# Chunked attention, a balanced mixture of experts and a float64 second layer on one core: weights are loaded two decodes ahead and decoded in even steps, the head hands over its x operands a step later, and the operands move by 352 bytes

## The chip, the cores and the metric

The kernel runs on one core of a Trainium2 chip. The metric is device time in microseconds (us) from the first to the last instruction and the little that lies around them; lower is better. Three runs of the kernel before stand beside one profiled execution of it.

## The reference

Three stages follow one another. Attention works in chunks of 64 positions; its output, as 2304 tokens of 512 features, goes through eight experts with a weight for every token and expert that eight rounds of row and column normalisation balance; a last layer takes the maximum of three products.

```python
def _attn_ref(q, k, v):                      # (4, 8, 576, 64), chunks of 64
    scores = scale * np.matmul(q_c, k_c.transpose(0, 1, 2, 4, 3))
    attn = np.exp(scores - scores.max(-1, keepdims=True))
    return np.matmul(attn / (attn.sum(-1, keepdims=True) + 1e-09), v_c)

def _moe_ref(x, w_gate, w1, w2):             # x (2304, 512), 8 experts, hidden 1024
    logits = x @ w_gate
    P = np.exp(logits - logits.max())
    for _ in range(8):
        P /= P.sum(1, keepdims=True) + 1e-09
        P /= P.sum(0, keepdims=True) + 1e-09
        P *= N / E
    for e in range(E):
        out += P[:, e:e + 1] * (np.maximum(x @ w1[e], 0.0) @ w2[e])

def _moe2_ref(x, w1, w2, w3, w_out):         # hidden 768
    h = np.maximum(np.maximum(x @ w1, x @ w2), x @ w3)
    return h @ w_out
```

The weights of the last layer (`wts2` in the kernel) reach the chip as 64-bit words, which are float64 numbers; the kernel decodes them itself into a high and a low float32 part.

## The kernel before

Every product is made of three matmuls of float32r halves: high by high, high by low, low by high (`wh`, `wl` for weights, `xh`, `xl` for tokens, `hh`, `hl` for hidden values). The first product of a layer is Strassen-like: seven products (`PRODUCTS`) in place of eight, so one item of work has 42 matmuls of 128x384 (line 235). The second product (`down`, line 267) has 36 matmuls of 128x512 for an expert item: six output tiles, each evicted by VectorE into `acc`.

An **item** is a pair of hidden blocks of an expert for a third of the tokens ("M"), or one of nine pieces of the last layer ("m"). The phases run in the order M0, M1, m0, M2, m1, m2 with 32, 32, 9, 32, 9 and 9 items, numbered through as n = 0 to 122. Within an item the seven products are the **positions** 0 to 6. After each position the main loop issues, in order of the code, the prepared side work of that place (the table `bg`, filled by `at(n, pos, f)`), then at position 1 the weight fetch of a later item (`fetch`, lines 166 to 170), and then one output tile of the item before. At position 2 `fetch2` (line 178) comes ahead of the side work. Every engine runs its own instructions strictly in that order, and all transfers are issued by SP, one after another: an entry of SP's queue that waits holds all behind it.

In the first 49 us, the **head**, a loop over k = 0 to 7 makes attention for the first six tiles: scores (`s`), exponentials (`e`), normalisation (lines 491 to 494), transposes on TensorE (`tp`), the product with v (`xp`), and from each two tiles an `x_head` call, which makes 128 columns of `xh` and `xl`. `warm` issues matmuls on ones, whose result nobody reads.

Side work that the change touches: `fold_all` (items 22 to 30) loads 30 stored partial sums (`u`) three steps ahead and adds them into `acc` (line 322). `decode_all` makes the operands of the last layer from the float64 words in 24 jobs during items 33 to 62: one or two loads of `w`, three empty steps, ten arithmetic steps on VectorE (first reader of `w` is line 383, tile `sc`), the high half `dhi` by ScalarE, the low half `dlo` by GpSimd, and two stores of them into `scr` (line 423) or `scro` (line 437). Ten steps fall into one item. From item 33 on, a third buffer for `wh` and `wl`, in the pool `late` at the other end of the memory, serves every third item.

Of the kernel before, what the change touches and what calls it, by code (L numbers as in the profile page):

```python
# [47 lines left out]
def kernel(ctx: ExitStack, tc: tile.TileContext, qk, vv, wg, wts, wts2, out):  # L48
# [24 lines left out]
    cp.tile([P, 392], F32, name="gap")  # L73
# [239 lines left out]
    def fold_all():  # L313
        jobs = [(e, t) for e in range(NRAW) for t in range(TS)]
        got = {}
        for i in range(len(jobs) + 3):
            if i < len(jobs):
                got[i] = big[0].tile([P, DM], F32, name="u", tag="u", bufs=4)
                nc.sync.dma_start(out=got[i], in_=up_part[jobs[i]])
            if i >= 3:  # L320
                e, t = jobs[i - 3]
                nc.vector.scalar_tensor_tensor(out=acc[t], in0=got.pop(i - 3), scalar=Pt[:, t, e:e + 1],
                                               in1=acc[t], op0=ALU.mult, op1=ALU.add)
            yield
# [24 lines left out]
    def x_head(j, r):  # L349

        cols = slice(j * P, (j + 1) * P)
        tt = nc.vector.tensor_tensor
        T = ap_.tile([P, 4, 2, P], F32, name="xT", tag="xT", bufs=1)
        tt(out=T[:, 0], in0=r[:, 1, 0:2], in1=r[:, 0, 0:2], op=ALU.subtract)
        tt(out=T[:, 1], in0=r[:, 1, 2:4], in1=T[:, 0], op=ALU.subtract)
        tt(out=T[:, 2], in0=r[:, 1, 2:4], in1=r[:, 1, 0:2], op=ALU.subtract)
        tt(out=T[:, 3], in0=r[:, 0, 2:4], in1=T[:, 1], op=ALU.subtract)
        nc.scalar.copy(out=xh[:, 0:2, :, cols], in_=r[:, 0].rearrange("p (i k) q -> p i k q", i=2))
        nc.scalar.copy(out=xh[:, 2, :, cols], in_=r[:, 1, 2:4])
        nc.scalar.copy(out=xh[:, 3:7, :, cols], in_=T)  # L360
        nc.gpsimd.tensor_tensor(out=xl[:, 0:2, :, cols], in0=r[:, 0].rearrange("p (i k) q -> p i k q", i=2),  # L361
                                in1=xh[:, 0:2, :, cols].bitcast(F32), op=ALU.subtract)
        nc.gpsimd.tensor_tensor(out=xl[:, 2, :, cols], in0=r[:, 1, 2:4], in1=xh[:, 2, :, cols].bitcast(F32),
                                op=ALU.subtract)
        for i in range(2):
            c = slice(3 + 2 * i, 5 + 2 * i)
            tt(out=xl[:, c, :, cols], in0=T[:, 2 * i:2 * i + 2], in1=xh[:, c, :, cols].bitcast(F32), op=ALU.subtract)  # L367
# [4 lines left out]
    def decode(srcs):  # L372
        T = lambda dt, nm: big[0].tile([P, 512], dt, name=nm, tag=nm)
        w = big[0].tile([P, 512, 2], I32, name="w64", tag="big")
        for place, src in srcs:
            o = w.rearrange("p (i f) x -> p i (f x)", i=4)[:, place]
            nc.sync.dma_start(out=o, in_=src)
        yield
        yield
        yield  # L380
        lo32, hi32 = w.bitcast(U32)[:, :, 0], w[:, :, 1]
        sc = T(I32, "sc")
        nc.vector.tensor_scalar(out=sc, in0=hi32, scalar1=20, scalar2=0x7FF,
                                op0=ALU.logical_shift_right, op1=ALU.bitwise_and)
        nc.vector.tensor_scalar(out=sc, in0=sc, scalar1=-896.0, scalar2=0.0, op0=ALU.add, op1=ALU.max)
        yield
        nc.vector.tensor_scalar(out=sc, in0=sc, scalar1=255.0, scalar2=float(1 << 23), op0=ALU.min, op1=ALU.mult)
        yield
        nc.vector.scalar_tensor_tensor(out=sc, in0=hi32, scalar=-(1 << 31), in1=sc,
                                       op0=ALU.bitwise_and, op1=ALU.bitwise_or)  # L390
        yield
        m = T(I32, "mant")
        nc.vector.tensor_single_scalar(out=m, in_=hi32, scalar=0xFFFFF, op=ALU.bitwise_and)
        yield
        v = T(F32, "val")
        nc.vector.tensor_scalar(out=v, in0=m, scalar1=float(1 << 20), scalar2=2.0 ** -20, op0=ALU.add, op1=ALU.mult)
        scf = sc.bitcast(F32)
        yield
        nc.vector.tensor_tensor(out=v, in0=v, in1=scf, op=ALU.mult)
# [3 lines left out]
        yield (v, r)  # L403

    def decode_all():
        for p in range(NP2):
            for i in range(3):
                for k in range(2):
                    of = lambda h: wts2[2 * (2 * p + h) + i // 2, :, i % 2].rearrange(
                        "p (k f) -> p k f", k=KD)[:, k::2]  # L410
                    for got in decode([(slice(1, 3), of(0)), (slice(0, 4, 3), of(1))]):
                        yield
                    v, r = got
                    V = big[0].tile([P, 8, P], F32, name="V", tag="V")
                    nc.vector.tensor_tensor(out=V[:, 0:4].rearrange("p i f -> p (i f)"), in0=v, in1=r, op=ALU.add)
                    yield
                    strassen_w([V[:, x] for x in range(4)], [V[:, 4 + x] for x in range(4)], nc.vector)
                    yield
                    hi = big[0].tile([P, 7, P], F32R, name="dhi", tag="dhi")
                    lo = big[0].tile([P, 7, P], F32R, name="dlo", tag="dlo")  # L420
                    hilo(hi, lo, V[:, 1:8])
                    for x, h in ((hi, 0), (lo, 1)):
                        nc.sync.dma_start(out=scr[p * 3 + i, h, :, :, k, :], in_=x.bitcast(F32))
                    yield
            for c in range(2):
                for got in decode([(slice(0, 4), wts2[2 * (2 * p + c) + 1, :, 1].rearrange(
                        "p (i f) -> p i f", i=4))]):
                    yield
                v, r = got
                hi = big[0].tile([P, 7, P], F32R, name="dhi", tag="dhi")[:, 0:4].rearrange("p i f -> p (i f)")  # L430
                lo = big[0].tile([P, 7, P], F32R, name="dlo", tag="dlo")[:, 0:4].rearrange("p i f -> p (i f)")
                nc.scalar.copy(out=hi, in_=v)
                nc.vector.tensor_tensor(out=v, in0=v, in1=hi.bitcast(F32), op=ALU.subtract)
                yield
                nc.vector.tensor_tensor(out=lo, in0=v, in1=r, op=ALU.add)
                for x, h in ((hi, 0), (lo, 1)):
                    nc.sync.dma_start(out=scro[p, h, :, c], in_=x.bitcast(F32))
                yield

# [192 lines left out]
    for a in range(NPAIR + 1, first_of[2] - 1):  # L632
        for b in range(7):
            for _ in range(1 + b % 2):
# [3 lines left out]
    for i in range(NRAW * TS + 3):  # L638
# [16 lines left out]
    with tc.manual_schedule():  # L655
# [12 lines left out]
        warm(10)  # L668
        for k in range(NPE + 2):
# [12 lines left out]
            warm(4 if k < NPE else 8)  # L682
# [80 lines left out]
```

## Time and profile before

| | us |
|---|---|
| runs of the kernel before (median, lowest, highest of 3) | 1988.83, 1987.73, 1994.11 |
| profiled execution: its time | 1989.79 |
| profiled execution: its span, first to last instruction | 1988.0 |
| TensorE busy | 1899.8 (96%) |
| VectorE busy | 1140.0 (57%) |
| ScalarE busy, GpSimd busy | 674.2, 620.8 |
| granted TensorE clock, mean | 0.981 |

The busy share of TensorE is the share in which a matmul was in flight; matmuls overlap, so it is not the share of its peak. The clock is granted at one of two levels, 1.2 or 2.4 GHz, and 0.981 is the mean as a share of the upper one. Items are found in the trace by counting 42 matmuls of line 235 each.

### The profile page before, as it was taken

What the parts mean: (1) busy time and instruction counts of PE and PEld (TensorE: products, weight loads), DVE (VectorE), ACT (ScalarE), POOL (GpSimd) and SP (SyncE); (2) the same over time, 40 slices, a digit from 0 to 9 for tenths busy, and PEclk for the clock granted to TensorE, in tenths of its full rate; (3) what the DMA queues carried; (4) which work ended last, traced back from release to release, by engine and by line L of the source; (5) the groups of instructions that cost most, each with busy time, mean ns of one, the idle gap of its engine ahead of it and who ended that gap; (6) DMA issues with size and microseconds to landing.
All of it is one profiled execution on the core that took longest, in us unless ns stands there. A gap on an engine that the chain in (4) does not pass through costs nothing.

```text
span 1988.0 us, 26887 instructions
## 1 busy us (share of the span) xinstructions
PE 1899.8 (96%) x10401; PEld 1690.9 (85%) x10407; DVE 1140.0 (57%) x1786; ACT 674.2 (34%) x1167; POOL 620.8 (31%) x424
## 2 busy tenths in 40 slices
PE   6999999999999889999998999999999999999898
PEld 4888888888888778878877789888888888889897
DVE  6566555637874576766765663544454444453534
ACT  4554554454444222222222233332222222232221
POOL 3766666777871111111121111211111111120201
PEclk8999999999999999999998999999999999999999
DMA  6577867778986565665656847554444554546562
GB/s 243 179 271 284 316 249 281 275 275 303 325 317 251 208 242 207 240 247 207 242 175 233 279 166 275 203 210 180 175 175 187 197 198 176 206 167 258 200 248 91
DMA packets 172671, 455.29 MB, mean 229 GB/s; under 512 B 14464, under 2 KB 81024, under 8 KB 172544
## 3 DMA queue, kind: packets, MB, share of 16 engines
q1 hardware_dynamic: 172544, 453.58, 62.1%
q8 instruction: 82, 1.34, 0.3%
q14 instruction: 45, 0.37, 0.1%
HBM read 319.57 MB, written 132.38 MB: 227 GB/s over the span
## 4 chain that ended last, share of the span: by engine, by line
PE 79%; DVE 7%; DMA 6%; ACT 3%; issue 3%; POOL 2%; SPq 1%; DVEq 0%; ACTq 0%; POOLq 0%
PE dn L267 38%; PE pa L235 22%; PE pg L235 11%; PE pb L235 6%; DMA w2l<-w2s 3%; DMA w<-in_wts 3%; DVE c L243 1%; DVE acc L290 1%; POOL dlo L182 1%; PE gp L560 1%; ACT hh L211 1%; PE s L469 1%; PE xp L548 1%; ACT xh L181 0%; DVE hl L217 0%
## 5 line engine op out<-in xcount | busy, mean ns | idle before, releaser
L267 PE MATMUL dn<-w2h,hh 128*128 128x512 f32 x1260 | 501.6, 398 | 28.3 <-ACT hh L211 16.8
L267 PE MATMUL dn<-w2h,hl 128*128 128x512 f32 x1260 | 504.4, 400 | 5.7 <-DVE hl L217 5.0
L267 PE MATMUL dn<-w2l,hh 128*128 128x512 f32 x1260 | 501.3, 398 | 3.8 <-DMA w2l<-w2s 3.8
L290 DVE SCALAR_TENSOR_TENSOR acc<-dn,Pt,acc 128x512 f32<-128x512 f32 x438 | 327.0, 747 | 266.6 <-PE dn L267 264.9
L214 POOL TENSOR_TENSOR hl<-c,hh 128x768 fp32r<-128x768 f32 x96 | 177.7, 1851 | 884.6 <-ACT c L213 879.7
L235 PE MATMUL pa<-xh,wh 128*128 128x384 f32 x984 | 336.4, 342 | 22.2 <-DVE c L243 12.1
L235 PE MATMUL pa<-xl,wh 128*128 128x384 f32 x984 | 333.5, 339 | 0.5 <-POOL xl L361 0.5
L235 PE MATMUL pa<-xh,wl 128*128 128x384 f32 x984 | 332.5, 338 | 0.0
L211 ACT ACTIVATE hh<-c 128x768 fp32r<-128x768 f32 x192 | 131.7, 686 | 521.5 <-DVE c L243 521.3
L267 PEld LDWEIGHTS dn<-w2h,hh 128*128 128x128 f32 x1260 | 239.5, 190 | 63.3 <-ACT hh L211 18.7
L267 PEld LDWEIGHTS dn<-w2h,hl 128*128 128x128 f32 x1260 | 238.6, 189 | 62.1 <-DVE hl L217 8.6
L267 PEld LDWEIGHTS dn<-w2l,hh 128*128 128x128 f32 x1260 | 238.7, 189 | 36.1 <-DMA w2l<-w2s 6.3
L235 PEld LDWEIGHTS pa<-xh,wh 128*128 128x128 f32 x984 | 186.4, 189 | 41.7 <-DVE c L243 16.6
L240 ACT COPY s<-pa 128x384 f32<-128x384 f32 x246 | 118.0, 480 | 247.0 <-PE pa L235 246.8
L235 PEld LDWEIGHTS pa<-xl,wh 128*128 128x128 f32 x984 | 186.5, 190 | 13.5 <-POOL xl L361 0.9
L235 PEld LDWEIGHTS pa<-xh,wl 128*128 128x128 f32 x984 | 186.2, 189 | 0.0
L235 PE MATMUL pg<-xh,wh 128*128 128x384 f32 x492 | 167.8, 341 | 4.8 <-DVE c L243 3.7
L235 PE MATMUL pg<-xl,wh 128*128 128x384 f32 x492 | 168.3, 342 | 0.4 <-DVE xl L367 0.4
L235 PE MATMUL pg<-xh,wl 128*128 128x384 f32 x492 | 167.3, 340 | 0.0
L217 DVE SCALAR_TENSOR_TENSOR hl<-c,hh 128x384 fp32r<-128x384 f32 x96 | 114.3, 1191 | 60.3 <-ACT hh L211 59.1
L243 DVE TENSOR_TENSOR c<-pb,s 128x384 f32<-128x384 f32 x114 | 63.1, 553 | 97.2 <-PE pb L235 91.9
L240 ACT COPY s<-pg 128x384 f32<-128x384 f32 x123 | 59.1, 481 | 169.1 <-PE pg L235 168.8
(126 smaller groups left out, 2366.3 us busy)
## 6 DMA issues: line engine op xcount, KB each, us to landing
wh<-w1s SPq DMA_DIRECT2D x64, 896.0 KB, 4.7
wl<-w1s SPq DMA_DIRECT2D x64, 896.0 KB, 7.2
w2h<-w2s SPq DMA_DIRECT2D x64, 512.0 KB, 8.3
w2l<-w2s SPq DMA_DIRECT2D x64, 512.0 KB, 9.1
w1s<-wh SPq DMA_DIRECT2D x32, 896.0 KB, 7.6
w1s<-wl SPq DMA_DIRECT2D x32, 896.0 KB, 9.3
wh<-scr SPq DMA_DIRECT2D x27, 896.0 KB, 4.6
wl<-scr SPq DMA_DIRECT2D x27, 896.0 KB, 6.5
```

The source lines that it names most:

```text
L182: (eng or nc.gpsimd).tensor_tensor(out=l, in0=v, in1=h.bitcast(F32), op=ALU.subtract)
L211: nc.scalar.activation(out=hh[:, q], in_=src, func=AF.Relu)
L214: nc.gpsimd.tensor_tensor(out=hl[:, q], in0=src, in1=hh[:, q].bitcast(F32), op=ALU.subtract)
L217: nc.vector.scalar_tensor_tensor(out=hl[:, q], in0=src, scalar=0.0, in1=hh[:, q].bitcast(F32), op0=ALU.max, op1=ALU.subtract)
L235: nc.tensor.matmul(ps, lhsT=x[:, wi, ws], rhs=y[:, xi, k], start=b not in begun, stop=k == 1 and i == 2, skip_group_check=True)
L240: nc.scalar.copy(out=s[pos], in_=ps)
L243: nc.vector.tensor_tensor(out=c[:, q], in0=ps, in1=s[other], op=ALU.add)
L267: nc.tensor.matmul(p, lhsT=h[:, hi, ts], rhs=w[:, f, :], start=(f == 0 and i == 0), stop=(f == 1 and i == 2))
L290: nc.vector.scalar_tensor_tensor(out=acc[t], in0=p, scalar=Pt[:, t, e:e + 1], in1=acc[t], op0=ALU.mult, op1=ALU.add)
L469: nc.tensor.matmul(ss[g][cs, hp, :], lhsT=a[r, hp, 0, cs], rhs=a[r, hp, 1, cs], start=True, stop=True)
L548: nc.tensor.matmul(p[64 * g:64 * g + 64, hp, :].rearrange("p (a q) -> p a q", a=2), lhsT=v[r, h * D:(h + 1) * D], rhs=aT[r, :, he, :], sta ...
L560: nc.tensor.matmul(p, lhsT=x[:, k, :], rhs=wgr[:, k, :], start=k == 0, stop=k == KD - 1)
```

## The change

`decode_all` loads the words of a job two jobs before it decodes them, into a tag `ld` with three buffers (which `fold_all` now uses too, with a lead of two steps in place of three). The empty steps are gone; a job is nine steps (eight for the output matrix), and eight steps fall into one item in place of ten, one per position and two at position 3. The tile `scm` for the exponent and mantissa now shares the one buffer of the tag `dhi`. One VectorE instruction (line 396) becomes a ScalarE activation; the output matrix's low half goes to GpSimd. The stores come one step after the step that makes the halves. In the head the four subtractions of `x_head` go to GpSimd for the first two calls, the last two subtractions on VectorE come one k later, `prep(0, 2)` and `raw2(1)` move from k = 2 to 3, and 8 + 8 warming matmuls after k = 6 and 7 become 12 at the end. The tile `gap` grows by 352 bytes: the built program has `xh` at byte 20480 of a partition before and 20832 after, and `xl`, `wh`, `wl`, `w2h`, `w2l`, `hh` and `hl` move with it; the pool `late` stays at 215008.

```diff
-    cp.tile([P, 392], F32, name="gap")
+    cp.tile([P, 480], F32, name="gap")
...
-        for i in range(len(jobs) + 3):
+        for i in range(len(jobs) + 2):
             if i < len(jobs):
-                got[i] = big[0].tile([P, DM], F32, name="u", tag="u", bufs=4)
+                got[i] = big[0].tile([P, 2 * DM], F32, name="u", tag="ld", bufs=3)[:, 0:DM]
                 nc.sync.dma_start(out=got[i], in_=up_part[jobs[i]])
-            if i >= 3:
-                e, t = jobs[i - 3]
+            if i >= 2:
+                e, t = jobs[i - 2]
...
-    def x_head(j, r):
+    def x_head(j, r, eng):
...
+            eng.tensor_tensor(out=o, in0=a, in1=b, op=ALU.subtract)
+        yield
...
-    def decode(srcs):
-        T = lambda dt, nm: big[0].tile([P, 512], dt, name=nm, tag=nm)
-        w = big[0].tile([P, 512, 2], I32, name="w64", tag="big")
+    def decode_load(srcs):
+        w = big[0].tile([P, 512, 2], I32, name="w64", tag="ld", bufs=3)
         for place, src in srcs:
             o = w.rearrange("p (i f) x -> p i (f x)", i=4)[:, place]
             nc.sync.dma_start(out=o, in_=src)
-        yield
-        yield
-        yield
+        return w
+
+    def decode(w):
+        scm = big[0].tile([P, 2, 512], I32, name="scm", tag="dhi")
...
+        nc.scalar.activation(out=v, in_=m, func=AF.Copy, scale=2.0 ** -20, bias=1.0)
...
-        v = T(F32, "val")
-        nc.vector.tensor_scalar(out=v, in0=m, scalar1=float(1 << 20), scalar2=2.0 ** -20, op0=ALU.add, op1=ALU.mult)
...
+        for at_ in range(-2, len(jobs)):
+            if at_ + 2 < len(jobs):
+                loaded[at_ + 2] = decode_load(jobs[at_ + 2][3])
+            if at_ < 0:
+                yield
+                continue
+            p, i, k, _ = jobs[at_]
+            for got in decode(loaded.pop(at_)):
+                yield
...
+            yield
+            for x, h in ((hi, 0), (lo, 1)):
+                nc.sync.dma_start(out=dst(h), in_=x.bitcast(F32))
...
-            for _ in range(1 + b % 2):
+            for _ in range(1 + (b == 3)):
                 at(a, b, lambda: next(dec, None))
...
-            warm(4 if k < NPE else 8)
+            warm(4 if k < NPE else 0)
...
-            if k == 2:
+            if k == 3:
                 prep(0, 2)
                 raw2(1)
+            if xg:
+                next(xg.pop(0))
             if k >= 3 and k % 2:
-                x_head(k // 2 - 1, raw_t[k // 2 - 1])
+                g = x_head(k // 2 - 1, raw_t[k // 2 - 1], nc.gpsimd if k < NPE else nc.vector)
+                next(g)
+                next(g)
+                xg.append(g)
+        next(xg.pop(0))
+        warm(12)
```

What stands on VectorE at the beginning of a decode job, before the change (the fifth job, in item 38; `w` is the tile of 64-bit words, `V` the decoded block of the job before, `c` and `acc` the path of the matmul results):

```order
L122 TENSOR_TENSOR V<-V 128x128
L123 TENSOR_TENSOR V<-V 128x128
L124 TENSOR_TENSOR V<-V 128x128
L125 TENSOR_TENSOR V<-V 128x128
L290 SCALAR_TENSOR_TENSOR acc<-dn,Pt,acc 128x512 x3
L243 TENSOR_TENSOR c<-pb,s_7007 128x384
L383 TENSOR_SCALAR sc<-w_7035 128x512
L385 TENSOR_SCALAR sc<-sc 128x512
L290 SCALAR_TENSOR_TENSOR acc<-dn,Pt,acc 128x512
```

And with the change, at the third job (item 35):

```order
L122 TENSOR_TENSOR V<-V 128x128
L123 TENSOR_TENSOR V<-V 128x128
L124 TENSOR_TENSOR V<-V 128x128
L125 TENSOR_TENSOR V<-V 128x128
L290 SCALAR_TENSOR_TENSOR acc<-dn,Pt,acc 128x512
L243 TENSOR_TENSOR c<-pb,s_6595 128x384
L388 TENSOR_SCALAR scm<-w_6357 128x512
L290 SCALAR_TENSOR_TENSOR acc<-dn,Pt,acc 128x512
```

The first reader of the words (line 388) has moved nearer to the end of the job before: one eviction in place of three lies between. It now writes the buffer from which the job before stores `dhi`, so it waits for the landing of that store as well as for the words.

SP's queue in the same stretch, before (`scr` the store of a job's halves, `wh` to `w2l` the fetch for an item):

```order
L423 DMA scr<-dhi 896x1x128
L423 DMA scr<-dlo 896x1x128
L377 DMA w_7035<-in_wts 128x2x256 x2
L170 DMA wh<-w1s 128x1792
L170 DMA wl<-w1s 128x1792
```

And with the change:

```order
L447 DMA scr<-dhi 896x1x128
L447 DMA scr<-dlo 896x1x128
L381 DMA w_6520<-in_wts 128x2x256 x2
L170 DMA wh<-w1s 128x1792
L170 DMA wl<-w1s 128x1792
```

The sequence is the same; but the words that SP loads there are those of the job after the next, and the two stores stand one position later than the step that makes their data.

On VectorE in the head, before (`xT` the four subtractions, `xl` the low halves, lines 491 on the normalisation of the next tile):

```order
L479 TENSOR_TENSOR e<-s,nm 128x2x128
L354 TENSOR_TENSOR xT<-xr 128x256
L355 TENSOR_TENSOR xT<-xr,xT 128x256
L356 TENSOR_TENSOR xT<-xr 128x256
L357 TENSOR_TENSOR xT<-xr,xT 128x256
L367 TENSOR_TENSOR xl<-xT,xh 128x4x128 x2
L491 TENSOR_REDUCE sm<-e 128x8
```

And with the change, on VectorE at the next k, and on GpSimd:

```order
L503 TENSOR_TENSOR e<-e,sm 128x512
L487 TENSOR_REDUCE nm<-s 128x4
L488 TENSOR_TENSOR e<-s,nm 128x2x128
L487 TENSOR_REDUCE nm<-s 128x4
L488 TENSOR_TENSOR e<-s,nm 128x2x128
L370 TENSOR_TENSOR xl<-xT,xh 128x4x128 x2
L500 TENSOR_REDUCE sm<-e 128x8
```

```order
L182 TENSOR_TENSOR w2l<-sw,w2h 128x4x4x32 x2
L355 TENSOR_TENSOR xT<-xr 128x256
L355 TENSOR_TENSOR xT<-xr,xT 128x256
L355 TENSOR_TENSOR xT<-xr 128x256
L355 TENSOR_TENSOR xT<-xr,xT 128x256
L360 TENSOR_TENSOR xl<-xr,xh 128x4x128
```

The subtractions have left VectorE and follow the `w2l` pair on GpSimd; the two `xl` instructions stand behind one more tile's normalisation and scores.

## Rows read from the trace of the kernel before

**Rows 1.** Stretches: us, busy us (x count) by engine, granted clock, DMA share, GB/s.

```profile
390.63:593.95 203.32, 203.32 (x1016) 182.75 (x1015) 138.85 (x174) 94.82 (x151) 159.52 (x113) 1.00 0.83 308
613.27:1167.18 553.91, 510.11 (x2425) 447.49 (x2424) 360.81 (x632) 151.65 (x253) 99.93 (x51) 0.96 0.63 224
```

**Rows 2.** VectorE's waits, 613.27 to 1167.18: us in total, times, longest.

```profile
DVE sc L383 <- DMA w<-in_wts: 106.2, 19, 11.4
```

**Rows 3.** TensorE's waits in the same stretch.

```profile
PE dn L267 <- ACT hh L211: 15.7, 2, 8.7
PE pa L235 <- DVE c L243: 12.1, 9, 2.7
PE dn L267 <- DVE hl L217: 5.0, 6, 1.1
...
PE dn L267 <- DMA w2l<-w2s: 3.8, 6, 0.7
```

**Rows 4.** Timeline of VectorE, first reader of the words, idle time in brackets.

```profile
650.81 0.43 DVE L383 TENSOR_SCALAR sc<-w 128x512 int32<-128x512 int32 x1 [9.68 <-DMA w<-in_wts]
...
718.82 0.43 DVE L383 TENSOR_SCALAR sc<-w 128x512 int32<-128x512 int32 x1 [6.20 <-DMA w<-in_wts]
...
848.51 0.43 DVE L383 TENSOR_SCALAR sc<-w 128x512 int32<-128x512 int32 x1 [4.39 <-DMA w<-in_wts]
```

**Rows 5.** Timeline of SP's queue around one job's stores.

```profile
687.43 0.53 SPq L423 DMA_DIRECT2D scr<-dhi  x1
689.69 0.51 SPq L423 DMA_DIRECT2D scr<-dlo  x1
...
693.11 0.70 SPq L178 DMA_DIRECT2D w2l<-w2s  x1
```

**Rows 6.** DMA issues: count, KB each, median us from issue to landing.

```profile
w2l<-w2s SPq DMA_DIRECT2D x64, 512.0 KB, 9.1
...
w<-in_wts SPq DMA_DIRECT2D x36, 256.0 KB, 4.4
...
scr<-dhi SPq DMA_DIRECT2D x18, 448.0 KB, 3.0
```

**Rows 7.** Tile dhi in 964 to 980, one store issued behind a fetch.

```profile
DMA to landing us min/median/max: 5.6/5.6/5.6
```

**Rows 8.** Critical chain in phase M2: start us, us, what.

```profile
1301.67 2.08 PE pa L235 x12
1303.76 1.39 PE dn L267 x6
...
1317.31 2.11 PE pa L235 x12
...
1333.04 2.10 PE pa L235 x12
```

**Rows 9.** Timeline of VectorE in the head.

```profile
20.78 1.69 DVE L494 TENSOR_TENSOR e<-e,sm 128x512 f32<-128x512 f32 x1
...
26.78 1.82 DVE L367 TENSOR_TENSOR xl<-xT,xh 128x512 fp32r<-128x512 f32 x2 [1.26 <-ACT xh L360]
...
29.67 0.69 DVE L494 TENSOR_TENSOR e<-e,sm 128x512 f32<-128x512 f32 x1
```

**Rows 10.** Timeline of TensorE at the end of the head.

```profile
42.89 1.09 PE L503 MATMUL tp<-ident,e 128*128 128x128 f32 x4 [4.45 <-DVE e L494]
43.77 2.96 PE L653 MATMUL warm<-wones 128*128 128x512 bf16 x8
...
49.16 0.53 PE L235 MATMUL pa<-xh,wh 128*128 128x384 f32 x1
```

**Rows 11.** Timeline of GpSimd in the head.

```profile
10.00 0.75 POOL L122 TENSOR_TENSOR ws<-st 128x256 f32<-128x256 f32 x1 [8.70 <-DMA st<-in_wts]
...
20.66 2.95 POOL L182 TENSOR_TENSOR w2l<-sw,w2h 128x512 fp32r<-128x512 f32 x2 [3.65 <-ACT w2h L181]
```

**Rows 12.** Timeline of SP, loads of partial sums.

```profile
480.13 1.36 SPq L319 DMA_DIRECT2D u<-upart  x3
```

**Rows 13.** Timeline of VectorE, the partial sum that those loads are nearest to.

```profile
484.47 1.22 DVE L322 SCALAR_TENSOR_TENSOR acc<-u,Pt,acc 128x512 f32<-128x512 f32 x1
```

More of the change, by code (lines that the diff above doesn't have):

```diff
@@ L366, in x_head @@
             c = slice(3 + 2 * i, 5 + 2 * i)
-            tt(out=xl[:, c, :, cols], in0=T[:, 2 * i:2 * i + 2], in1=xh[:, c, :, cols].bitcast(F32), op=ALU.subtract)
+            nc.scalar.copy(out=xh[:, c, :, cols], in_=T[:, 2 * i:2 * i + 2])
+        yield
+        for i in range(2):
+            c = slice(3 + 2 * i, 5 + 2 * i)
+            nc.vector.tensor_tensor(out=xl[:, c, :, cols], in0=T[:, 2 * i:2 * i + 2],
+                                    in1=xh[:, c, :, cols].bitcast(F32), op=ALU.subtract)
+        yield
     big = [None]
-    def decode(srcs):
-        T = lambda dt, nm: big[0].tile([P, 512], dt, name=nm, tag=nm)
-        w = big[0].tile([P, 512, 2], I32, name="w64", tag="big")
+    def decode_load(srcs):
+        w = big[0].tile([P, 512, 2], I32, name="w64", tag="ld", bufs=3)
         for place, src in srcs:
@@ L402, in decode @@
         nc.vector.scalar_tensor_tensor(out=r, in0=lo32, scalar=2.0 ** -52, in1=scf, op0=ALU.mult, op1=ALU.mult)
-        yield (v, r)
+        yield
+        nc.vector.tensor_tensor(out=v, in0=v, in1=scf, op=ALU.mult)
+        yield (V, v, r)
     def decode_all():
+        jobs = []
         for p in range(NP2):
@@ L410, in decode_all @@
                         "p (k f) -> p k f", k=KD)[:, k::2]
[L411 to L424, printed above, removed]
-            for c in range(2):
[L426 to L433, printed above, removed]
+                    jobs.append((p, i, k, [(slice(1, 3), of(0)), (slice(0, 4, 3), of(1))]))
@@ L434, in decode_all @@
+            for c in range(2):
+                jobs.append((p, None, c, [(slice(0, 4), wts2[2 * (2 * p + c) + 1, :, 1].rearrange(
+                    "p (i f) -> p i f", i=4))]))
+        loaded = {}
+        for at_ in range(-2, len(jobs)):
+            if at_ + 2 < len(jobs):
+                loaded[at_ + 2] = decode_load(jobs[at_ + 2][3])
+            if at_ < 0:
                 yield
-                nc.vector.tensor_tensor(out=lo, in0=v, in1=r, op=ALU.add)
-                for x, h in ((hi, 0), (lo, 1)):
-                    nc.sync.dma_start(out=scro[p, h, :, c], in_=x.bitcast(F32))
+                continue
+            p, i, k, _ = jobs[at_]
+            for got in decode(loaded.pop(at_)):
@@ L438, in decode_all @@
                 yield
+            V, v, r = got
+            nc.vector.tensor_tensor(out=V[:, 0:4].rearrange("p i f -> p (i f)"), in0=v, in1=r, op=ALU.add)
+            hi = big[0].tile([P, 7, P], F32R, name="dhi", tag="dhi")
+            lo = big[0].tile([P, 7, P], F32R, name="dlo", tag="dlo")
+            yield
+            if i is not None:
+                strassen_w([V[:, x] for x in range(4)], [V[:, 4 + x] for x in range(4)], nc.vector)
+                yield
+                hilo(hi, lo, V[:, 1:8])
+                dst = lambda h: scr[p * 3 + i, h, :, :, k, :]
+            else:
+                hi, lo = (x[:, 0:4].rearrange("p i f -> p (i f)") for x in (hi, lo))
+                hilo(hi, lo, V[:, 0:4].rearrange("p i f -> p (i f)"))
+                dst = lambda h: scro[p, h, :, k]
@@ L441 @@
+            yield
+            for x, h in ((hi, 0), (lo, 1)):
+                nc.sync.dma_start(out=dst(h), in_=x.bitcast(F32))
     att = ExitStack()
@@ L637 @@
     f0 = 4 * NRAW + 2
-    for i in range(NRAW * TS + 3):
+    for i in range(NRAW * TS + 2):
         at(f0 + i // 4, (0, 2, 4, 5)[i % 4], lambda: next(folds, None))
@@ L668 @@
         warm(10)
+        xg = []
         for k in range(NPE + 2):
```

29 lines of the change are left out of this document (12 added, 17 removed).

## The prediction, made before the changed kernel ran

> **What bounds the kernel now.** TensorE is busy 96% of the span, so I read first what an undisturbed item costs, then where items cost more. The table of stretches gives the undisturbed pace: 390.63 to 593.95 is 13 items, 15.64 us each, with TensorE in flight for all of it [rows 1]. The stretch from the first to the last decode, 613.27 to 1167.18, holds 31 items (n = 33 to 63), which at 15.64 would take 485 us; it takes 553.91. **68 us** are lost there (a further 1 us is the slower third item, below). 44 us of them are idle time of TensorE (553.91 - 510.11); the other 24 go with the granted clock, 0.96 in the mean in place of 1.00: TensorE falls to the lower level after its longer waits [rows 1]. The list of waits names the cause: VectorE stands 106.2 us, 19 times, at line 383, waiting for the 64-bit words [rows 2], and TensorE waits 15.7 + 12.1 + 5.0 us for results that VectorE makes or ScalarE makes from them, and 3.8 us for `w2l` [rows 3]. So decode blocks VectorE, and the evictions and sums behind the blocked instruction are what TensorE lacks.
>
> Why the words are late: the load is issued only behind the two stores of the job before, and the store of `dlo` waits for GpSimd; in [rows 5] the stores stand at 687.43 and 689.69. Then the load itself takes 4.4 us in the median [rows 6]; three empty steps are about three positions of 2.4 us (half of 2.08 and 1.39, [rows 8]) less the doubled ones. Transfers queue: where a load was issued behind a fetch, VectorE waited 9.68 us, and a store issued behind a fetch landed after 5.6 us in place of the usual 3.0 [rows 4, 6, 7].
>
> **Decode, loads two jobs ahead.** This removes the wait for the words: two jobs of eight or nine steps, 15.64 / 8 = 2 us each, lie between load and use, some 34 us, against 10 us of waiting at worst [rows 4]. What is late next is the store. Line 388 writes the buffer from which the previous job's `dhi` is stored, so each of 23 job starts waits for that landing, at best 3.0 us after issue [rows 6]. I go by the position of the start, with the eight steps of an item laid on the positions 0, 1, 2, 3, 3, 4, 5, 6 and nine or eight steps a job.
>
> Starts at positions 4 to 6 (8 of 23): the item's fetch, issued at its start and landed 9 to 10 us later [rows 6], is over. ScalarE's copy runs about a position before the use, so of 3.0 us some 1 to 3 us are left as a stall. Starts at position 3 (7): the store is queued behind the fetch and lands about 12 us into the item (fetch end 10.6 plus its own 1.3; estimate from 9.1, [rows 6], and the four issues in front); VectorE arrives at about 9.5 (three positions of 2.4, a product and an addition): 2.4 us. Starts at position 2 (2): arrival 5.7, stall 6.2. Starts at positions 0 and 1 (6): stalls of 3 to 4 us, harmless for VectorE, but here the fetch stands behind stores and loads in SP's queue: from the store of `dhi` to the issue of `w2l` 5.7 us [rows 5], landing some 10 later, which is 18 us (position 0) or 20 (position 1) into an item whose successor needs it at about 17. Together some 62 us of stall in place of 106.
>
> What a stall costs TensorE depends on its length. Eleven of the 19 stalls are over 6 us, 81 us in sum, and two of the eleven stand in [rows 4]; the others are 4.4 or less, and behind the one of 4.39 at 848.51 no wait of TensorE over 0.3 us follows. So I charge 0.8 for each us of a long stall and 0.1 for a short one: 12 x 0.8 + 50 x 0.1 = 15. The six late fetches cost 4 x 1.2 + 2 x 3.5 = 12, with the clock 15. **Loss after 30, gain 38.** Bounds: a gain of 68 if all of it is covered, and of 17 if each of the 23 starts costs 2.2 us.
>
> Other edits of decode: the instruction that goes to ScalarE took 0.4 us of VectorE, 24 times; both engines have idle time there [rows 1], so nothing either way; its ScalarE form is not in the trace, nearest is the copy of 0.6 us for the same shape. If that cover were gone, it would be 10 us.
>
> **Head.** The wait of TensorE before a transpose is 4.45 us where `x_head` stands on VectorE between scores and normalisation [rows 10]: four subtractions, a wait of 1.26 for ScalarE and two instructions of 1.82 together [rows 9]. For the first two calls the subtractions now run on GpSimd, 0.75 each for that shape, behind the `w2l` pair of 2.95 at the first [rows 11]; ScalarE's copies wait for them, and the exponentials of the next tile stand behind these copies. So I give the first call 1 us and the second, which has no `w2l` in front, 3. The eight warming matmuls of 2.96 us leave the path between the last transpose and the last product with v [rows 10], and twelve come behind it, 3 to 4.4 us at the two rates seen, where eight stood. I take the start of item 0 at 45 to 47 in place of 49.16 and the waits for `xh` and `xl` in it as partly gone: **gain 5**, bounds 0 and 9.
>
> A rule speaks against this part. [rows 9] show VectorE's line 494 at 1.69 us at 20.78, while GpSimd ran `w2l` from 20.66 [rows 11]; without company it takes 0.69 at 29.67 [rows 9]. The Trainium skill, SBUF — State Buffer, section Who interferes with whom, says that a VectorE instruction with two SBUF inputs and a GpSimd one that reads SBUF exclude each other for their whole length; this trace agrees. By the row alone, eight subtractions of 0.75 us could hold VectorE for 6 us more; that is the rival below.
>
> **Partial sums.** With a lead of two steps the three loads at 480.13 [rows 12] serve first the addition at 484.47 [rows 13]; a load of 256 KB takes 4.4 us or a little more [rows 6], so VectorE stands about 1 us in each of nine items. TensorE is in flight throughout there [rows 1]: cost 0, and 9 us if that cover were gone.
>
> **The 352 bytes.** In phase M2 every third item takes 15.73 in place of 15.64 us, and its first twelve matmuls 2.11 in place of 2.08 [rows 8]; these have their weights in `late`, whose address is off a multiple of 64 by 32, while all other operands lie on multiples of 512. After the move all are off by 32. Either the relative place counts (then `late` gets in step: gain of 0.1 x 30, 3 us), or the absolute one (then all other items pay: 93 x 0.1, and with the second product's weights 78/42 of that, 17 us). I take 0 between them, since no row tells them apart. The Trainium skill, SBUF — State Buffer, section Specifications, gives 16-byte lines as the unit; both places are multiples of 16, so by it neither would matter. The row of `late` already contradicts it.
>
> **Sum.** 1989.79 - 38 - 5 + 0 = 1946.8 for a profiled execution; that one stood 0.96 above the median of the runs, so 1946.
>
> **Rivals.** (1) The store takes the place of the load. For it: line 388 waits for it in 23 jobs and the queue is the same. Against: it is one transfer of 3.0 us, not two behind two stores. Each start costs 2.2 us: gain 17 + 5, **1967**. (2) The absolute address counts: 1946 + 17, **1963**. For it: the row of `late`; against: `late` also differs in its place relative to `xh`. (3) GpSimd's subtractions hold VectorE: head 1 us worse than now, **1952**. (4) Slower: if VectorE falls behind, each store is issued into the fetch and every start stalls as the two at position 2, 23 x 6.2 = 143 us; at the mean price of 68/106 that is a loss of 91 in place of 68, less 5 in the head: **2007**. It decides from a mean stall of 4.9 us a start. Against: the mean I find is 2.7. (5) The words were not what held VectorE, and the wait moves whole to the store: **1984** (head alone). Against: [rows 2] name the load 19 times.
>
> **Chances.** Forecast 0.58 with its own range of 1925 to 1957; (1) 0.14; (2) 0.12; (3) 0.05; (4) 0.06; (5) 0.05. The range 1924 to 1969 takes in the forecast, (2), (3) and most of (1) and leaves out (4), (5) and a gain near the full 68. A change of 0.3%, 6 us, is about what a measurement of this kernel can tell from none: faster 0.91 (all but (4) and part of (5)), same 0.03, slower 0.06.
>
> **What would show it.** The stretch of items 33 to 63 at about 516 us in place of 554, with VectorE's wait at the first reader of `scm` naming `scr<-dhi` at some 60 us; `w<-in_wts` gone from the waits; TensorE waiting for `w2h` or `w2l` after jobs that begin at positions 0 and 1; item 0 beginning at 45 to 47; undisturbed items at 15.64. I am wrong if those items change their pace, if the store's wait is over 110 us, or if item 0 begins after 49.

## The result, and the profile after

The changed kernel takes **1934.87 us** in the median of four runs (1933.78 to 1935.99), the kernel before 1988.67 beside it: a ratio of 0.9724, 95% interval 0.9706 to 0.9742. The forecast was 1946 with a range of 1924 to 1969. The profiled execution took 1934.4 us with a span of 1932.6, in place of 1989.79 and 1988.0.

The difference of 55.4 us between the two spans lies in two places. Where items begin and end, by counting 42 matmuls of line 235 each:

| stretch, us | before | after |
|---|---|---|
| start to item 0 (the head) | 49.16 | 45.16 |
| item 0 | 13.47 | 9.42 |
| items 1 to 32 | 550.64 | 550.56 |
| items 33 to 63 (decode) | 553.91 | 505.66 |
| item 64 to the end | 820.79 | 821.82 |

Decode gives 48.3 us and the head with item 0 gives 8.0; the rest gives back 1. The table of stretches of the kernel after, for item 0, for the stretch without decode that answers to the first of [rows 1], and for items 33 to 63, which answer to its second (columns as there):

```profile
45.16:54.58 9.42, 9.42 (x60) 9.39 (x59) 2.87 (x5) 5.20 (x10) 7.03 (x6) 0.99 0.34 117
...
382.55:585.87 203.32, 203.32 (x1015) 182.75 (x1015) 136.28 (x174) 94.80 (x151) 159.75 (x113) 1.00 0.82 308
605.15:1110.80 505.65, 494.24 (x2425) 438.69 (x2423) 342.18 (x602) 167.82 (x277) 108.30 (x57) 0.99 0.69 246
```

The undisturbed pace is the same to the hundredth: 203.32 for 13 items, 15.64 each. At that pace the 31 decode items would take 484.8, so 20.8 us are still lost there, in place of 68: 11.4 of them are idle time of TensorE. The granted clock, 0.99 in the mean in place of 0.96, accounts for about 3.4 more: it is 0.91 in item 41, 0.92 in item 44 and 1.00 in every other one. The remaining 6 are time in which TensorE counts as in flight at the upper clock.

What VectorE waits for at the first reader of the words in the same stretch, as in [rows 2] (us in total, times, longest):

```profile
DVE scm L388 <- DMA scr<-dhi: 40.9, 15, 4.8
...
DVE scm L388 <- issue: 8.3, 3, 3.7
DVE scm L388 <- DMA w<-in_wts: 7.4, 1, 7.4
DVE scm L388 <- POOL dlo L182: 5.2, 3, 2.0
...
DVE scm L388 <- DMA scro<-dhi: 3.4, 2, 1.9
```

The words hold VectorE only at the first job, whose load is two steps old. At the other 23 starts it waits 57.8 us in sum. At 17 of them the trace names the store of `dhi` of the job before, at six something that ends near it; with a buffer of its own for `scm` all 23 waits are gone (e4). What reaches TensorE of it is little, as its waits in the stretch show, beside [rows 3]:

```profile
PE dn L267 <- DMA w2h<-w2s: 3.7, 2, 2.4
PE dn L267 <- DVE hl L217: 3.4, 5, 1.0
PE dn L267 <- DMA w2l<-w2s: 2.8, 4, 0.7
PE dn L267 <- ACT hh L211: 1.4, 3, 0.5
```

The largest single losses are now late fetches. The costliest item is number 44 with 20.85 us. SP's queue in the item before it, which begins at 768.88, and at the beginning of item 44:

```profile
772.69 0.52 SPq L447 DMA_DIRECT2D scr<-dhi  x1
774.95 0.52 SPq L447 DMA_DIRECT2D scr<-dlo  x1
775.56 1.66 SPq L381 DMA_DIRECT2D w<-in_wts  x2
777.31 0.45 SPq L170 DMA_DIRECT2D wh<-w1s  x1
...
778.29 0.52 SPq L178 DMA_DIRECT2D w2h<-w2s  x1
...
784.59 0.32 SPq L170 DMA_DIRECT2D wh<-w1s  x1
```

And the row of TensorE that waits for the `w2h` of 778.29, 9.9 us after its issue:

```profile
788.21 0.47 PE L267 MATMUL dn<-w2h,hh 128*128 128x512 f32 x1 [2.43 <-DMA w2h<-w2s]
```

The store of `dhi` is issued 3.81 us into the item, when ScalarE has made its data, and that of `dlo` 2.26 us later, since it waits for GpSimd. The words' load and the fetch stand behind both, so the fetch begins 8.4 us into the item; the next one, with no store in front of it, begins with its item, at 784.59. The table of TensorE's waits has two such waits for `w2h`. In both items the clock falls as well (0.91 and 0.92, above), and items 41 and 44 together cost 9.3 us.

In the head, the rows of TensorE that answer to [rows 10]:

```profile
15.69 0.66 PE L512 MATMUL tp<-ident,e 128*128 128x128 f32 x4 [0.16 <-ACT xr L549]
...
28.59 1.11 PE L512 MATMUL tp<-ident,e 128*128 128x128 f32 x4 [6.28 <-ACT xr L549]
...
37.48 0.66 PE L512 MATMUL tp<-ident,e 128*128 128x128 f32 x4 [1.59 <-ACT xr L549]
...
40.82 4.77 PE L662 MATMUL warm<-wones 128*128 128x512 bf16 x11 [0.34 <-issue]
```

The wait of 4.45 at the second call has become 1.59. At the first call it has become longer, 6.28, and names ScalarE. The rows of ScalarE there say why:

```profile
26.28 0.62 ACT L366 CAST xh<-xT 128x512 fp32r<-128x512 f32 x1 [3.19 <-POOL xT L355]
27.65 0.62 ACT L366 CAST xh<-xT 128x512 fp32r<-128x512 f32 x1 [0.75 <-POOL xT L355]
28.17 0.64 ACT L549 COPY xr<-xp 128x256 f32<-128x256 f32 x2
```

The copy for which TensorE waits stands in order behind two copies that wait for GpSimd's subtractions, and these stand behind the `w2l` pair. The tail is longer by 1.4 (6.27 us from the last transposes to item 0 before, 7.68 after). What brings item 0 forward beside the second call is the first row: the second group of transposes begins at 15.69 behind a wait of 0.16, where in the kernel before it begins behind one of 3.95:

```profile
17.70 1.08 PE L503 MATMUL tp<-ident,e 128*128 128x128 f32 x4 [3.95 <-DVE e L494]
```

VectorE was the cause, by these rows of the kernel before,

```profile
12.95 1.79 DVE L492 TENSOR_SCALAR sm<-sm 128x8 f32<-128x8 f32 x1
...
15.01 2.55 DVE L494 TENSOR_TENSOR e<-e,sm 128x512 f32<-128x512 f32 x1
```

which stand beside two `wl` subtractions of GpSimd, and which take 0.28 and 0.69 us in the kernel after. The change does not touch these instructions. Over all runs the beginning of item 0 goes with the beginning of this second group: in the ten profiles with the new head it is 45.2 to 45.7 where the group begins by 16.4, 46.8 to 47.0 where it begins at 17.0, and 48.07 where it begins at 18.03. The three profiles with the old head have the group at 17.46 to 17.70 and item 0 at 49.2 to 49.3. So the new head may have a part in moving it; no run separates that.

### The profile page after: what moved, and what is told of

Same layout as the page of the kernel before. It is cut to its first block, busy times and chain, and to the rows that moved or that the text cites. A ratio compares the mean times of both kernels' runs of the same rounds, so it can differ in the third digit from the quotient of the medians.

```text
span 1932.6 us, 26875 instructions
## 1 busy us (share of the span) xinstructions
PE 1882.9 (97%) x10397; PEld 1681.6 (87%) x10403; DVE 1116.0 (58%) x1748; ACT 690.7 (36%) x1194; POOL 636.1 (33%) x438
## 4 chain that ended last, share of the span: by engine, by line
PE 88%; DVE 4%; DMA 4%; ACT 3%; issue 1%; POOL 1%; SPq 0%; DVEq 0%; ACTq 0%; POOLq 0%
PE dn L267 42%; PE pa L235 24%; PE pg L235 12%; PE pb L235 6%; DMA w2l<-w2s 2%; DMA scr<-dhi 1%; PE s L478 1%; PE gp L569 1%; DVE c L243 1%; PE warm L662 1%; ACT hh L211 1%; PE xp L557 1%; DVE acc L290 1%; DVE xl L182 1%; DVE hl L217 0%
## 5 line engine op out<-in xcount | busy, mean ns | idle before, releaser
L217 DVE SCALAR_TENSOR_TENSOR hl<-c,hh 128x384 fp32r<-128x384 f32 x96 | 109.0, 1135 | 60.6 <-ACT hh L211 59.4
```

The costliest lines, as they stand in the source:

```text
L217: nc.vector.scalar_tensor_tensor(out=hl[:, q], in0=src, scalar=0.0, in1=hh[:, q].bitcast(F32), op0=ALU.max, op1=ALU.subtract)
```

## The experiments

Eleven kernels, each beside its own runs of the kernel before on the same chip (medians 1988.51, 1989.35, 1989.47 and 1989.31). "Stretch" is items 33 to 63 of the profiled run. The decode code of the changed kernel stands unaltered in three of the profiles and gave 505.66, 501.44 and 504.63, so a difference of about 4 us between stretches says nothing. Diffs are against the changed kernel, but for the last.

| run | time, us | ratio to before, 95% | stretch |
|---|---|---|---|
| changed kernel | 1934.87 | 0.9724 (0.9706 to 0.9742) | 505.66 |
| e1, load late | 1965.48 | 0.9884 (0.9865 to 0.9903) | 537.56 |
| e2, address as before | 1935.55 | 0.9729 (0.9709 to 0.9749) | 501.44 |
| e3, head as before | 1942.56 | 0.9771 (0.9749 to 0.9792) | 504.63 |
| e4, own buffer for scm | 1925.9 | 0.9693 (0.9663 to 0.9722) | 496.90 |
| e5, e4 and stores behind the fetch | 1914.51 | 0.9634 (0.9608 to 0.966) | 486.00 |
| e6, stores a step earlier | 1939.07 | 0.975 (0.9726 to 0.9774) | 510.10 |
| e7, e1 and e6 | 1975.3 | 0.9935 (0.991 to 0.996) | 548.52 |
| e8, one job of lead | 1930.94 | 0.9713 (0.9689 to 0.9736) | 500.66 |
| e9, ten steps to an item | 1949.74 | 0.9804 (0.9778 to 0.983) | 522.16 |
| e10, e5 with the load late | 1915.94 | 0.963 (0.9609 to 0.9651) | 485.98 |
| e11, kernel before, stores behind the fetch | 1930.16 | 0.9704 (0.9679 to 0.973) | 494.12 |

**e1: the words loaded at their own job's start, as before.**

```diff
-        for at_ in range(-2, len(jobs)):
-            if at_ + 2 < len(jobs):
-                loaded[at_ + 2] = decode_load(jobs[at_ + 2][3])
...
+        for at_ in range(len(jobs)):
+            loaded[at_] = decode_load(jobs[at_][3])
+            yield
+            yield
+            yield
...
-            for _ in range(1 + (b == 3)):
+            for _ in range(1 + b % 2):
```

> The changed kernel with the words loaded again at the start of their own job, with three empty steps before the first reader and ten steps an item as before; the shared tile, the ScalarE activation, the later stores, the head and the addresses stay. Theory (the words' early load is what brought the 48 us of the decode stretch): VectorE waits for w<-in_wts again for 70 us or more and the time goes back by 35 to 48 us, to 1970 to 1983. Rival (the stores, which stand one step later and no longer hold up the fetch in SP's queue, and the lighter VectorE brought it): at most 15 us slower than the changed kernel, 1935 to 1950.

Between the two: 1965.48. The words' wait is back (VectorE 82.7 us, 18 times), but the stretch loses 31.9 of the 48.3 us, not all. The edit brings back the ten uneven steps to an item together with the late load; the steps alone cost 16.5 with the early load kept (e9), so the 31.9 are the price of both. What else in the change is worth 16, e6 and e7 look for.

**e2: `gap` back to 392.**

> The changed kernel with the operands at their old addresses. Theory (only the place of the third weight buffer relative to the others counts): every third item after n = 32 takes 15.75 in place of 15.70 us, some 30 items, so 1 to 2 us slower, 1936 to 1937, and undisturbed items stay at 15.64. Rival (the absolute address counts too, or the move hid a loss elsewhere): 15.64 changes, or the difference is over 4 us.

No difference in time that can be told. The chain of this kernel in phase M2, first matmuls of an item with `late` and of the next one (start, us):

```profile
1305.85 2.11 PE pa L235 x12
...
1321.58 2.10 PE pa L235 x12
```

and of the changed kernel:

```profile
1308.59 2.10 PE pa L235 x12
...
1324.27 2.10 PE pa L235 x12
```

The item with `late` takes 15.73 in the first, as before [rows 8], and 15.68 in the second. Counted by matmuls it is 15.75 and 15.70, the others 15.64 in both. So all other operands may lie 32 bytes off at no cost, and the place relative to them is worth 0.05 us for each of some 30 items, 1.5 us. The item with `late` stays 0.06 us over the others even so; no run shows why.

**e3: the head as before** (`x_head`, `prep`, `raw2` and the warming matmuls).

> The changed kernel with the head of the kernel before: the four subtractions on VectorE in the same k, the old place of prep and raw2, 8 and 8 warming matmuls. Theory (the head's edits brought all of the 8 us by which item 1 begins earlier, and nothing later gives it back): 1942 to 1944, item 1 begins at 62 to 63. Rival (part of it came from elsewhere, for example from the addresses or the clock's phase): under 1940.

1942.56, as the theory had it: item 0 begins at 49.22 and takes 13.46 again. The head is worth 8 in time. All ten profiles with the new head have item 0 at 9.3 to 9.6 us; its beginning lies between 45.16 and 48.07.

**e4: `scm` in a buffer of its own.**

```diff
-        scm = big[0].tile([P, 2, 512], I32, name="scm", tag="dhi")
+        scm = big[0].tile([P, 2, 512], I32, name="scm", tag="big")
```

> The changed kernel with the tile scm in a buffer that no store reads (the tag big, idle during the decode), so that the first reader of the words waits for no store. Theory (the waits for the store are 2 to 5 us each, 57 us in sum, and TensorE's slack covers nearly all of them; what is left of the loss is the late fetch): 2 to 8 us faster, 1927 to 1933, with the waits of TensorE for w2h and w2l still there. Rival (the store's wait holds most of the 21 us still lost in the decode stretch): 14 us faster or more, 1921 or less.

VectorE's wait for the store is gone, and with it 8.8 us of the stretch; the time, 1925.9, is a little under the theory's, and its interval just overlaps that of the changed kernel. Single items bear the 8.8 out: items 35, 36, 37, 46, 48, 55, 56 and 57, which take 0.6 to 1.6 us more than 15.64 in the changed kernel, take at most 0.06 more here; item 54, in which a fetch is late here, goes the other way, from 1.1 to 4.0. TensorE still waits for fetches:

```profile
PE dn L267 <- DMA w2h<-w2s: 3.7, 2, 2.4
PE dn L267 <- DMA w2l<-w2s: 2.1, 3, 0.7
```

**e5: e4, and the two stores of a job are kept in a list that is issued at positions 2 to 4 only, behind the item's fetch.**

```diff
+    def flush():
+        while stores:
+            to, x = stores.pop(0)
+            nc.sync.dma_start(out=to, in_=x.bitcast(F32))
...
-                nc.sync.dma_start(out=dst(h), in_=x.bitcast(F32))
+                stores.append((dst(h), x))
...
+            if b in (2, 3, 4):
+                at(a, b, flush)
```

> The kernel with scm in its own buffer, and with the two stores of a job issued only at positions 2 to 4 of an item, that is always behind the item's weight fetch in SP's queue. Theory (what is left in the decode stretch is the fetch that stands behind stores whose data are not ready): the waits of TensorE for w2h and w2l vanish, the stretch of items 33 to 63 falls from 497 to 486 to 489, and the time to 1914 to 1919. Rival (the fetch is late because the words' loads and the stores fill the DMA engines): the waits for w2h and w2l stay and the time is within 4 us of 1926.

As expected: 1914.51, the best of all, and TensorE is in flight for the whole stretch:

```profile
605.82:1091.82 486.00, 486.00 (x2426) 437.14 (x2424) 360.66 (x602) 168.26 (x277) 108.80 (x57) 1.00 0.72 256
```

So the loss of 20.8 us in the changed kernel splits into 8.8 for the store's wait (e4), 10.9 for fetches behind stores (e4 to e5), and 1.2 that stays; the first two are known to some 4 us, by how far stretches of one code differ.

**e6: the stores in the step that makes the halves, as before; e7: this with the late load of e1.**

```diff
-            yield
             for x, h in ((hi, 0), (lo, 1)):
                 nc.sync.dma_start(out=dst(h), in_=x.bitcast(F32))
+            yield
```

> The changed kernel with the stores in the same step as the halves that they store, as before the change; all else stays. Theory (16 of the 48 us come from the stores that stand a step later, so that SP is held for a shorter time ahead of a fetch): the stretch of items 33 to 63 goes from 506 to 512 to 522 and the time to 1941 to 1951. Rival (those 16 us come from the shorter and steadier work of VectorE): no more than 3 us slower.

> The kernel with the late load (words loaded at the start of their own job, three empty steps, ten steps an item), and with the stores in the step that makes the halves, as in the kernel before; the shared tile, the ScalarE activation, the head and the addresses stay as changed. Theory (late load and early store together are the loss of the kernel before): the stretch of items 33 to 63 takes 548 to 556 as before, the time 1976 to 1984. Rival (the lighter VectorE and the three-buffer tag carry the 16 us that the late load alone left): the stretch stays at 534 to 541, the time at 1962 to 1969.

e6 lies between its two theories, 4.4 us above the changed kernel, which is no more than profiles of one code differ by. In e7 the same edit costs 11.0 over e1 (548.52 against 537.56), where the stretch falls into the theory's range and the time just under it. So the later store matters where the load is late, and the load's lead, the eight even steps and the later store together are 43 of the 48 us.

**e8: words loaded one job ahead** (`range(-1, ...)` and `at_ + 1`).

> The changed kernel with the words loaded one job ahead in place of two. Theory (a load that takes 4 to 11 us is covered by one job of 16 to 18 us): no change beyond 3 us, 1932 to 1938, and no wait of VectorE for the words after the first job. Rival (the second job of lead is needed, because SP issues the load only behind the stores and the fetch): VectorE waits for the words again in several jobs, 5 us slower or more.

1930.94, just under the theory, its interval overlapping that of the changed kernel: the second job of lead is worth nothing. VectorE waits for words only at the first job (6.6 us).

**e9: ten steps to an item, at uneven places, loads two jobs ahead.**

```diff
-            for _ in range(1 + (b == 3)):
+            for _ in range(1 + b % 2):
```

> The changed kernel with ten decode steps in an item, as before, in place of eight; loads stay two jobs ahead and jobs stay nine steps long. Theory: the pace by itself matters little, since each of 24 jobs still starts with one wait for the store of the job before (57.8 us over 23 starts now) and a few fetches still stand behind stores; 1931 to 1939 us, items 33 to 63 at 501 to 511 us in place of 505.66. Rival: even steps are a part of the gain, because two steps in one position put more of VectorE's work ahead of an eviction; then the stretch is 515 or more and the time 1944 or more.

The rival holds in its numbers: 1949.74. The stretch of this kernel:

```profile
605.52:1127.68 522.16, 500.51 (x2425) 442.26 (x2424) 341.45 (x602) 167.00 (x277) 108.21 (x57) 0.98 0.67 238
```

and TensorE's waits for `w2h` in it:

```profile
PE dn L267 <- DMA w2h<-w2s: 5.8, 6, 2.1
```

VectorE's waits for the store are hardly more (62.8 us in place of 57.8), but they lie otherwise. A job of nine steps now begins in the first 10 us of an item at 21 of 24 starts, where store and fetch meet; `w2h` is late six times in place of two, and two stalls of 5.2 and 6.0 us come just behind the beginning of an item. That two steps in one position put more work ahead of an eviction, the rival's reason, no row shows. So the eight even steps are a part of the gain as long as stores stand in front of fetches; the next run has ten uneven steps without that, and they cost nothing.

**e10: e5 with the late load and ten uneven steps of e1.**

> The version of 1914.51 us (own buffer for scm, stores issued at positions 2 to 4 only) with the words loaded at the start of their own job behind three empty steps, ten steps to an item. Theory: a load needs its lead whatever stands in front of it, since it takes 4.4 us by itself and some 10 behind a fetch, against three empty steps of 1.6 us each; VectorE waits 50 us or more for the words, items 33 to 63 take 510 us or more in place of 486.00, and the time is 1938 or more. Rival: the words were late only through the stores in front of them; then VectorE waits under 25 us for them, the stretch takes 495 or less and the time is 1924 or less.

The theory falls, wholly: with the stores behind the fetch, VectorE waits 6.9 us for words, at the first job alone, and the stretch is that of e5:

```profile
608.33:1094.31 485.98, 485.98 (x2426) 437.08 (x2424) 343.75 (x602) 169.05 (x277) 108.09 (x57) 1.00 0.72 256
```

SP's queue shows what I had not thought of. The load of one job:

```profile
692.47 5.15 SPq L381 DMA_DIRECT2D w<-in_wts  x2
```

Its reader on VectorE runs at 708.56. The load stands three steps ahead of it in the code, but SP issued it 16.1 us ahead: with the stores behind the fetch, SP runs ahead of the other engines until a buffer is not yet free, and most of its waiting in the stretch is now at the fetch, for TensorE to release a weight buffer:

```profile
SPq L170 <- PE pa L235: 215.5, 30, 13.7
```

Over the 23 jobs behind the first the load is issued 9.4 to 19.3 us ahead of its reader, in e1 4.3 to 6.7. In e1 the store of `dlo` stood at 715.67, the load behind it at 716.28, and the reader at 721.58 had waited 6.34 us.

**e11: the kernel before, with `flush` alone** (the list and its three positions as in e5; late load, ten steps, old head and old address).

> The kernel before, with one thing alone: the two stores of a decode job are issued only at positions 2 to 4 of an item, behind the item's fetch; words loaded at the start of their own job, ten uneven steps to an item, the old head. Theory: what made the words late was the store of dlo, which waits for GpSimd in SP's queue ahead of the load; with it out of the way SP runs ahead, VectorE waits under 15 us for words, items 33 to 63 take 486 to 492 us in place of 553.91, and the time is 1918 to 1928. Rival: the two extra steps between load and reader, or the lead itself, are needed in the older code; VectorE still waits 40 us or more for words, the stretch takes 510 or more and the time is 1945 or more.

1930.16, with 60 of the 68 us of loss gone: 2 us over the theory's range in time and in stretch, far from the rival's. VectorE still waits 25.8 us for words where the theory had under 15. The stretch, and that wait:

```profile
613.66:1107.78 494.12, 488.26 (x2426) 436.92 (x2425) 359.04 (x632) 154.89 (x253) 100.35 (x51) 1.00 0.72 251
```

```profile
DVE sc L383 <- DMA w<-in_wts: 25.8, 6, 7.5
```

The longest of these waits is where the stores at position 2 still stand directly in front of a load, on SP:

```profile
879.71 0.53 SPq L410 DMA_DIRECT2D scr<-dhi  x1
883.22 0.52 SPq L410 DMA_DIRECT2D scr<-dlo  x1
883.85 1.20 SPq L377 DMA_DIRECT2D w<-in_wts  x2
```

and on VectorE:

```profile
889.83 0.43 DVE L383 TENSOR_SCALAR sc<-w 128x512 int32<-128x512 int32 x1 [7.50 <-DMA w<-in_wts]
```

## Why the prediction was right, and where its sizes were off

**What bounds the kernel: right, and confirmed from both sides.** The words were late because the load stood behind stores that wait for their data. The change goes round that: with the load early the wait falls away, and the late load with ten steps costs 31.9 us (e1). Taking the stores out of the way does it too, in the kernel before by itself (e11), and then the lead is worth nothing (e10 against e5). So the early load is one remedy; the cause is the place of the stores in SP's queue. Of the two stores I had named the lesser, that of `dlo`. SP's waits at both in the kernel before, 613.27 to 1167.18:

```profile
SPq L423 <- ACT dhi L181: 111.1, 9, 18.2
SPq L423 <- ACT s L240: 80.5, 5, 16.3
SPq L437 <- ACT dhi L432: 59.9, 6, 14.4
SPq L423 <- ACT hh L211: 57.0, 4, 15.6
...
SPq L423 <- POOL dlo L182: 31.7, 18, 2.9
SPq L437 <- DVE dlo L435: 13.4, 6, 3.9
```

SP stands 308.5 us, 24 times, at the store of `dhi` for ScalarE and 45.1 us, 24 times, at that of `dlo`. No run moves one of the two alone.

**Decode: gain 38 forecast, 48.3 measured.** The mechanism held: the wait passed to the landing of `dhi`, 57.8 us over 23 starts where I had 62, and short stalls hardly reach TensorE. That the sum came so near is in part luck, for its parts did not come out so: the two starts at position 2 stall 3.2 us in place of 6.2, those in the first 5 us of an item 1.2 to 2.6 in place of 3 to 4, and the later ones up to 4.8. Two readings under it were wrong: the store of [rows 7] that landed after 5.6 us is one of the smaller ones into `scro`, whose other five land after 2.0 to 4.0, and one of the stalls that I gave as 4.4 or less was 5.04, at 871.23. Both terms of the loss that stays were too large. The stalls were put at 15, and e4 takes back 8.8: I had charged 0.8 for each us of the two starts at position 2, as if they were long ones, and they stall 3.2. The late fetches were put at 12, with the clock 15, over six items; e5 takes back 10.9 more, and in the changed kernel two items carry 9.3 of it, so this number too was met by other items than I had. Two edits that I gave no term of their own turned out to matter where the first obstacle stands: the later store (11 us with a late load, e7) and the eight steps (16.5 us, e9). With the stores behind the fetch, ten steps and a late load cost nothing (e10).

**Head: gain 5 forecast, 8.0 measured, by other terms.** Item 0 begins at 45.16, within 45 to 47. The second call's 3 was about right (2.9). The first lost 1.8 in place of gaining 1, through the `w2l` pair and ScalarE's order, which I had named, and the tail costs 1.4. That is about nothing, and most of the 4 us goes with the wait of 3.95 at 17.70, which I had not priced: there GpSimd's `wl` and VectorE's normalisation meet or miss each other. It is no firm gain: e10, with the same head, has that wait again, and item 0 at 48.07:

```profile
18.03 1.09 PE L518 MATMUL tp<-ident,e 128*128 128x128 f32 x4 [3.94 <-DVE e L509]
```

That item 0 began within my 45 to 47 is therefore luck in part. The firm half is item 0 itself, 13.47 to 9.42, where I had about 1. Its row in the kernel before (columns as in [rows 1]):

```profile
49.16:62.63 13.47, 11.44 (x61) 10.51 (x59) 5.78 (x7) 6.34 (x11) 10.25 (x9) 0.87 0.13 45
```

TensorE is idle for 2.0 us of it, in the waits for `xh` and `xl`; about 2 more go with the granted clock of 0.87. In e3, with the old head, it takes 13.46 at the same clock; in the kernel after it has no idle time and a clock of 0.99. The step that failed is the term of item 0: I took its waits as partly gone, where all of them went, and gave its clock no price.

**Partial sums and address: 0 and 0, right.** Items 1 to 32 take 550.56 in place of 550.64. The absolute address (17 us) falls with 203.32 for 13 items. The relative one is real but small, 1.5 us; the Trainium skill, SBUF — State Buffer, section Specifications, has lines of 16 bytes, by which neither place would matter, and the item with `late` differs all the same, 15.70 against 15.75 (e2).

**The rivals.** The store in the load's place (1967) happened, but at 8.8 us over 23 starts, 0.4 each, in place of 2.2. The slower case (2007) needed a mean stall of 4.9 us, and it is 2.5. That the words were not the cause (1984) falls with e1. GpSimd does hold VectorE in the head (1952), but less by the moved subtractions than by its own `xl` (lines 360 and 362), which it had before too. The two `xl` instructions of VectorE at line 370 take 2.91 us at the first call and 2.89 at the second, in place of 1.82 [rows 9]:

```profile
26.93 2.91 DVE L370 TENSOR_TENSOR xl<-xT,xh 128x512 fp32r<-128x512 f32 x2 [1.71 <-ACT xh L366]
...
36.98 2.89 DVE L370 TENSOR_TENSOR xl<-xT,xh 128x512 fp32r<-128x512 f32 x2
```

And GpSimd beside the second of them:

```profile
35.78 0.73 POOL L355 TENSOR_TENSOR xT<-xr,xT 128x256 f32<-128x256 f32 x1
36.46 1.72 POOL L360 TENSOR_TENSOR xl<-xr,xh 128x512 fp32r<-128x512 f32 x1
```

The last moved subtraction ends at 36.51, before the pair begins. No wait of TensorE for VectorE follows either pair. The Trainium skill, SBUF — State Buffer, section Who interferes with whom, has a VectorE instruction with two SBUF inputs and a GpSimd one that reads SBUF exclude each other; the traces agree, at line 370 with 1.1 us and at 15.01 in the kernel before with 1.9.

## What to carry to other kernels

Where a load comes late, look first at what stands in front of it in its queue, and there for an entry that waits for a compute engine: moving that entry behind the urgent transfers gave 60 us by itself in three places of the code, where all edits of the decode together gave 48. Before giving a load more lead in the code, compare the time of its issue with the time of its reader: once the stores stood behind the fetch, this queue ran ahead by itself (e10). And price the clock of the stretch behind a wait, not the wait alone: in item 0 it was worth as much as the waits.

## What the runs showed that I had not expected

SP issued a load 16.1 us ahead of its reader with three steps between them in the code (e10), and 5.3 us ahead where a waiting store stood in front (e1). VectorE's line 492 on 128x8 numbers took 1.79 us beside GpSimd's `wl` subtraction in the kernel before, though it has one input and few elements; in the changed kernel (line 501) it took 0.70 beside GpSimd's line 122 and 0.76 beside line 355, a moved subtraction, and 0.17 where no GpSimd instruction stood beside it. The first item behind the head ran at a granted clock of 0.99 in place of 0.87. In the kernel before the clock is 1.00 from 49.16 to 52.43 and 0.50 from 52.74 to 56.15, behind waits of 0.50 and 1.10 us within the item; in the changed kernel the item has no wait. Whether the waits or the twelve warming matmuls in front make the difference was not tried by itself. Items with every operand 32 bytes off took 15.64 us as before; an item with one set of weights alone 32 bytes off took 15.75, and 15.70 with all others moved by as much.
